# The first half of a retention and MLP kernel in rolling pairs of blocks, with 512-column first products

## The chip, the cores and the metric

The kernel runs on one core of one Trainium2 chip. The metric is the device time in microseconds, the median of three runs.

## The reference

Inputs q, k, v are (8, 8, 576, 64) in float32: 8 batches, 8 heads, 576 positions, 64 columns. The MLP has 512 inputs, 2048 hidden columns and 512 outputs.

```python
scores = q @ k.T / sqrt(64)                      # per batch and head
gamma  = 1 - 2 ** (-5 - head)
D      = gamma ** (i - j) where i >= j, else 0
attn   = (scores * D) @ v
x      = attn.transpose(0, 2, 1, 3).reshape(8 * 576, 8 * 64)   # (4608, 512)
h      = x @ w_in                                # (4608, 2048)
g      = maximum(h, 0) + alpha * minimum(h, 0)   # alpha per hidden column
out    = g @ w_out                               # (4608, 512)
```

The kernel must reach float32 accuracy. In the bulk of the work it gets there by splitting each float32 operand into three planes of a shorter format (`fp32r` in the profile), called planes 0, 1 and 2, and adding three products of planes.

## The kernel before

**Blocks, units, cells.** The 4608 tokens are 18 blocks (`kb`) of 256. The 2048 hidden columns are 8 units (`u`) of 256. A cell is one block by one unit: a first product (x by w_in, 512 deep, in four pieces `cc` of 128 and two halves `f` of 128 hidden columns), the activation with alpha, the split of g into planes, and a second product (g by w_out) that adds into PSUM. A visit is one block with four of the units; each block has two visits. The order is: blocks 0 to 15 with units 0 to 3 one block at a time (the first half), then blocks 16 and 17 in a pair, and then all blocks in pairs with units 4 to 7 (the second half). What the first visit of a block gives is stored to DRAM (`o_kept`, tile `ok`) and is added in the second.

**The start.** The first two batches' attention is computed with whole parts of q, k and v. The first eight cells (`unit_plain` L1073, `second_plain` L1104) work in plain float32 while the weights are loaded and converted (`convert`) and split (`split_w`).

**Attention beside the first half.** From the third batch on, attention goes by pairs of heads, 24 of them after the one of the start, one `joint` each. On TensorE a joint has the values of the pair before (L843, into `psh`) and the scores and state sums of its own pair (L895 and L902, L905, into `psh` and `psa`). Before it, `load_kq` and `load_kn` load q and k, `operands` scales them and turns them on VectorE (L821, into `kT` and `qT`; L826 scales `kn`). After it, VectorE masks the scores into `at` (L923) and forms the state sums (L937, L943, L946), and DMAs copy `qT` into `at` and the sums into `vn`. The x that comes out stays in a ring of five tiles `xs` and is stored to DRAM for the second visit (`fetch_x`). There are two rooms each of `kT`, `qT` and `kn`, and one of `kx`, `qx` and `at`.

**First half.** For a cell, `unit` makes per half `f` 12 matmuls of 256 columns (L1142) into one bank `psh[f]`: planes 0 and 1 into one half of the bank, plane 2 into the other. ScalarE and VectorE evacuate it in four steps into `ga` (L1149, L1150, L1153, L1156). `split_g` makes three planes of `ga` with two ScalarE (L1195, L1197) and two GpSimd passes (L1199, L1202). `second` makes 12 matmuls of 512 columns (L1275) into the four banks `pso`, two cells behind (`LAG`). `split_x` makes the planes of a block into one of two rooms `lx`, with four ScalarE and four GpSimd passes (L1030, L1045, L1048, L1052). Banks `psa` serve only the joints here.

**Second half.** `unit_two` makes the first product for two blocks at once: 12 matmuls of 512 columns (L1172) per half `f`, into the two banks `psh` for `f = 0` and `psa` for `f = 1`. It evacuates 512 columns at a time (L1178, L1179, L1182, L1184). The planes of x lie in the rooms that attention has left.

**The order of the work.** Every operation is recorded by `do` with its engine, a cost, what it reads and what it writes. Slots with a `Gen` for each use make an operation wait for all users of the room before. `plan` simulates the engines with these costs: first backwards for due times, then forwards, taking for each engine the ready operation that is due first. TensorE may run ahead in the recorded order by `AHEAD_PE` operations. The planner is called 144 times, 12 times on its own result and then with random changes to all due times, and the shortest plan is emitted. The order on each engine is then fixed; DMAs are nearly all issued on SP's queue (L208), in order, each waiting there for what it needs.

## Time and profile before

| what | value |
|---|---|
| median of 3 runs | 928.29 us (927.62 to 929.45) |
| profiled execution: span, first to last instruction | 926.8 us |
| profiled execution's own time | not listed apart; the span with 1.5 us around it is the median of the runs |
| mean granted TensorE clock | 0.999 |
| busy PE, PEld | 914.3 us (99%), 769.6 us (83%) |
| busy DVE, ACT, POOL | 521.1 us (56%), 542.6 us (59%), 601.9 us (65%) |
| DMA | 121.42 MB, mean 131 GB/s |
| L1142, first products of 256 columns | 1344 matmuls, 175.8 us busy |
| L1275, second products | 1608 matmuls, in two rows of 1392 and 216 |

PE is TensorE's matmuls, PEld its weight loads, DVE is VectorE, ACT is ScalarE, POOL is GpSimd, SP is the engine that issues DMAs. The profile gives times in microseconds, and the mean of one instruction in ns. Matmuls are pipelined, so that the mean of one is longer than the distance between two; for the distance take the length of a piece of the chain and divide by the number of matmuls. A row reads: line, engine, operation, output tile <- input tiles, shape, count, busy time, mean of one, and idle time before it with what ended it.

### The profile page before, as it was taken

Reading aid. Unit: us, or ns where it says so; the run is one execution under the profiler, and the core shown is the slowest. Engines: PE = TensorE matmul, PEld = TensorE weight load, DVE = VectorE, ACT = ScalarE, POOL = GpSimd, SP = SyncE. Lnnn points to the kernel's source line nnn. Section 1 sums busy time; section 2 is a strip of 40 time slices with the busy share of each in tenths; the row PEclk is TensorE's granted clock in tenths of the full one; section 3 lists DMA queues with packets and bytes.
Section 4 is the critical chain, followed back from the end, with each engine's and each line's share of the span. In section 5 each row is a group of like instructions: output and inputs, shape, how many; then the busy total and the mean of one; then the engine's idle time right before and its main releaser. Section 6 shows DMA issues by size and latency. Waiting matters only on the chain.

```text
span 926.8 us, 20611 instructions
## 1 busy us (share of the span) xinstructions
PE 914.3 (99%) x7913; PEld 769.6 (83%) x7913; DVE 521.1 (56%) x1043; ACT 542.6 (59%) x1164; POOL 601.9 (65%) x525
## 2 busy tenths in 40 slices
PE   7999999999999999999999999999999999999998
PEld 6666788888888888888988887888888888888886
DVE  7676666667676667666545454434454444443342
ACT  4566557567676667675856756545463646363442
POOL 4777856648776676674776678673756565565535
PEclk9999999999999999999999999999999999999999
DMA  9995687887988978964335231212121222311112
GB/s 225 247 228 105 168 190 156 197 192 167 205 209 201 212 172 207 197 148 134 116 123 165 86 114 45 92 46 92 46 91 58 80 82 76 106 56 47 46 46 68
DMA packets 235954, 121.42 MB, mean 131 GB/s; under 512 B 203456, under 2 KB 203728, under 8 KB 235856
## 3 DMA queue, kind: packets, MB, share of 16 engines
q1 hardware_dynamic: 235712, 119.98, 51.4%
q8 instruction: 62, 1.02, 0.5%
q14 instruction: 36, 0.29, 0.1%
q10 hardware_dynamic: 144, 0.13, 0.0%
HBM read 74.19 MB, written 32.51 MB: 115 GB/s over the span
## 4 chain that ended last, share of the span: by engine, by line
PE 92%; DMA 3%; DVE 1%; SPq 1%; POOL 1%; ACT 1%; issue 1%; POOLq 0%; ACTq 0%; DVEq 0%
PE pso L1275 39%; PE psh L1142 18%; PE psa L1172 11%; PE psh L1172 11%; PE psh L843 3%; PE pso L1104 2%; PE psh L1073 2%; PE psa L905 2%; SPq L208 1%; DMA w<-in_moe_w_out_dram 1%; PE psh L895 1%; PE psa L902 1%; DMA w<-in_v_dram 0%; DMA lx<-in_moe_w_in_dram 0%; DMA a<-in_moe_alpha_dram 0%
## 5 line engine op out<-in xcount | busy, mean ns | idle before, releaser
L1275 PE MATMUL pso<-w,g 128*128 128x512 f32 x1392 | 340.9, 391 | 0.6 <-POOL g L1202 0.6
L1275 PEld LDWEIGHTS pso<-w,g 128*128 128x128 f32 x1392 | 256.0, 188 | 51.5 <-POOL g L1202 1.2
L1202 POOL TENSOR_TENSOR g<-g 128x512 fp32r<-128x512 f32 x136 | 175.8, 1294 | 24.7 <-DVE w L1048 4.5
L1142 PE MATMUL psh<-lx,w 128*128 128x256 f32 x1344 | 175.8, 285 | 0.0
L1142 PEld LDWEIGHTS psh<-lx,w 128*128 128x128 f32 x1344 | 168.7, 191 | 6.9 <-issue 0.8
L1199 POOL TENSOR_TENSOR g<-ga,g 128x512 fp32r<-128x512 f32 x56 | 72.4, 1293 | 79.4 <-ACT g L1195 57.0
L1199 POOL TENSOR_TENSOR g<-x,g 128x512 fp32r<-128x512 f32 x48 | 62.2, 1296 | 73.7 <-ACT g L1195 55.7
L1149 ACT COPY ga<-psh 128x256 f32<-128x256 f32 x112 | 41.6, 372 | 57.2 <-PE psh L1142 54.4
L1199 POOL TENSOR_TENSOR g<-vn,g 128x512 fp32r<-128x512 f32 x32 | 41.5, 1295 | 40.5 <-ACT g L1195 34.3
L1150 DVE SCALAR_TENSOR_TENSOR ga<-psh,ga 128x256 f32<-128x256 f32 x112 | 47.2, 421 | 36.5 <-ACT ga L1149 34.5
L1156 DVE SCALAR_TENSOR_TENSOR ga<-psh,malpha,ga 128x256 f32<-128x256 f32 x112 | 53.4, 477 | 14.6 <-ACT psh L1153 14.0
L1153 ACT ACTIVATE psh<-ga 128x256 f32<-128x256 f32 x112 | 43.5, 388 | 22.6 <-DVE ga L1150 22.5
L1195 ACT ACTIVATE g<-x 128x512 fp32r<-128x512 f32 x48 | 30.3, 631 | 41.5 <-PE pso L1275 22.1
L1293 DVE TENSOR_TENSOR op<-pso,op 128x512 f32<-128x512 f32 x35 | 23.9, 687 | 52.9 <-PE pso L1275 52.9
L1275 PE MATMUL pso<-lx,g 128*128 128x512 f32 x216 | 52.0, 389 | 0.0
L1275 PEld LDWEIGHTS pso<-lx,g 128*128 128x128 f32 x216 | 40.5, 188 | 8.4
L923 DVE SCALAR_TENSOR_TENSOR at<-psa,pf,mask 64x512 f32<-64x512 f32 x48 | 36.0, 749 | 15.9 <-PE psa L902 14.9
L1195 ACT ACTIVATE g<-ga 128x512 fp32r<-128x512 f32 x56 | 35.4, 631 | 15.7 <-DVE ga L1156 14.7
L1048 POOL TENSOR_TENSOR lx<-x,lx 128x512 fp32r<-128x512 f32 x26 | 33.6, 1293 | 14.6 <-ACT lx L1045 9.8
L1179 DVE SCALAR_TENSOR_TENSOR x<-psh,x 128x512 f32<-128x512 f32 x24 | 16.5, 689 | 41.2 <-PE psh L1172 36.2
L1052 POOL TENSOR_TENSOR lx<-lx 128x512 fp32r<-128x512 f32 x28 | 36.2, 1294 | 2.5 <-DVE ga L1156 1.0
L843 PEld LDWEIGHTS psh<-at,vn 128*64 128x64 f32 x864 | 27.8, 137 | 10.6 <-issue 5.4
(311 smaller groups left out, 1842.4 us busy)
## 6 DMA issues: line engine op xcount, KB each, us to landing
xk<-x SPq DMA_DIRECT2D x18, 512.0 KB, 3.7
ok<-o SPq DMA_DIRECT2D x36, 256.0 KB, 2.6
op<-ok SPq DMA_DIRECT2D x18, 512.0 KB, 4.0
out_dram<-o SPq DMA_DIRECT2D x35, 256.0 KB, 2.3
x<-xk SPq DMA_DIRECT2D x16, 512.0 KB, 4.9
kx<-in_k_dram SPq DMA_DIRECT2D x96, 72.0 KB, 3.3
qx<-in_q_dram SPq DMA_DIRECT2D x96, 72.0 KB, 3.0
kn<-in_k_dram SPq DMA_DIRECT2D x48, 144.0 KB, 3.8
```

The source lines that it names most:

```text
L843: nc.tensor.matmul(pv[i].get()[half(h2), (j - js[0]) * C:(j - js[0] + 1) * C], vns[n % 2][:, h2, j], mt.get()[:, h2, j], start=True, stop= ...
L1052: lambda l=l, d=d, h=view(0, c): nc.gpsimd.tensor_tensor(out=piece(d()), in0=h(), in1=l(), op=ALU.subtract),
L1142: nc.tensor.matmul(at(b), w[:, c0:c0 + P], xp(l, cc), start=(n == 0 and cc == 0), stop=(n > 0 and cc == NCC - 1), skip_group_check=True)
L1149: do("ACT", 0.36, lambda g=g, at=at: nc.scalar.copy(g(), at(1)), [(ph, 1)], [(ga, f)])
L1150: do("DVE", 0.42, lambda g=g, at=at: nc.vector.scalar_tensor_tensor(out=g(), in0=at(0), scalar=ONE, in1=g(), op0=ALU.mult, op1=ALU.subtrac ...
L1153: do("ACT", 0.39, lambda g=g, at=at: nc.scalar.activation(at(1), g(), ACTF.Relu, scale=-1.0), [(ga, f)], [(ph, 1)])
L1156: do("DVE", 0.48, lambda g=g, at=at, fc=fc: nc.vector.scalar_tensor_tensor(out=g(), in0=at(1), scalar=malpha[:, fc:fc + 1], in1=g(), op0=A ...
L1172: nc.tensor.matmul(p.get(), w[:, c0:c0 + P], piece(words_of(g)[:, o:o + DM]), start=(l != 1 and cc == 0), stop=(l > 0 and cc == NCC - 1))
L1195: do("ACT", 0.64, lambda: nc.scalar.mul(piece(to.get()[:, 2]), whole(), BELOW), both, [(to, 2)])
L1199: do("POOL", 1.29, lambda: nc.gpsimd.tensor_tensor(out=piece(to.get()[:, 1]), in0=whole(), in1=to.get()[:, 2], op=ALU.subtract), both + [( ...
L1202: do("POOL", 1.29, lambda: nc.gpsimd.tensor_tensor(out=piece(to.get()[:, 2]), in0=to.get()[:, 0], in1=to.get()[:, 1], op=ALU.subtract), [( ...
L1275: nc.tensor.matmul(a[2 * m + b].get(), piece(g.get()[:, l, f, m * P:(m + 1) * P]), w_piece(u, 2 + f, l), start=(cell["first"] and f == 0 a ...
```

## The change

The blocks 2 to 15 of the first half go in rolling pairs. In step s (0 to 14) the blocks 1+s and 2+s are worked on with two units: units 0 and 1 in even steps, units 2 and 3 in odd ones. A block so gets two of its units as the newer one of a pair and two as the older one; in steps 0 and 14 there is one block alone. `unit_roll` makes the first product for both blocks at once, 512 columns per matmul, into `psh` for `f = 0` and `psa` for `f = 1`, in three operations of four matmuls. The two blocks' planes lie in one tile `lx` so that a matmul can take 256 columns of each with a fixed step between them. `split_roll` makes the planes with one ScalarE, one VectorE and one GpSimd pass per half of the block, and writes them into the room of the block two before. `acts_roll` evacuates 512 columns at a time.

`kT`, `qT` and `kn` get one room each, and `load_kn` moves from two pairs ahead to one. There are five rooms `ga` of 512 columns. The joints are placed by step (`JOINTS`). `split_g` has a second form (`quick`) with one ScalarE, one VectorE and one GpSimd pass, used in the last two steps, the first two pairs of the second half and at the very end. The later weight splits do one pass on VectorE in place of GpSimd (`WDVE`). The rooms of x and `ga` in the second half are chosen anew. The planner is called once, then 12 times on its own result, and then 243 times with random changes to the due times of operations within one stretch of 40 us at a time, keeping any plan that is no longer.

The core of the diff:

```diff
-    def plan(after=None):
-        after = after or [op.n for op in ops]
-
-        users = [[] for _ in ops]
+    users = []
+
+    def wait(d, op):
+        return 2.0 if d.late else 0.0 if d.eng == op.eng else LAT.get(d.eng, 0.1)
+
+    def dues(after):
...
+        return due
+
+    def plan(due):
...
+    WINDOWS, STRETCH, TRIES, ROUNDS = 27, 20.0, 9, 9
...
-    PUMP0, PUMP = ((1, 1), (0, 1), (0, 1), (0, 1)), ((1, 2), (1, 2), (0, 1), (0, 1))
+    X_TWO, QUICK, NQUICK, WDVE = 12, 13, 2, 16
+    PUMP_R = ((1, 1), (1, 1))
+    EARLY, JOINTS = 1, {(s, i): 1 for s in range(14) for i in range(2) if (s, i) not in ((0, 0), (8, 1), (10, 1), (13, 0), (13, 1))}
+    PUMP0, PUMP = ((1, 2), (0, 1), (0, 1), (0, 1)), ((1, 2), (1, 2), (0, 1), (0, 1))
...
-    lxs = [slot(lpool, f"lx{n}", [P, 3, NCC, TB]) for n in range(2)]
+    lx_tiles = {}
+
+    def lx_all(which):
+        if which not in lx_tiles:
+            lx_tiles[which] = lpool.tile([P, 6 * NCC, TB], FP32, tag="lx", name=f"lx_{which}")
+        return lx_tiles[which]
+
+    def lx_slots(which):
+        return [Slot(f"lx{n}", lambda n=n: lx_all(which)[:, 3 * NCC * n:3 * NCC * (n + 1)])
+                for n in range(2)]
+    lxs = lx_slots("w")
...
-    gas = [slot(mlp, f"ga{n}", [P, 2, TB]) for n in range(2)]
+    ga_all = mlp.tile([P, 5, DM], FP32, tag="ga", name="ga_all")
+    gas = [Slot(f"ga{n}", lambda n=n: ga_all[:, n].rearrange("p (f t) -> p f t", f=2)) for n in range(5)]
...
-    kns = [slot(nat, f"kn{n}", [P, NJ, D]) for n in range(2)]
-    kTs = [slot(attn, f"kT{n}", [P, S]) for n in range(2)]
-    qTs = [slot(attn, f"qT{n}", [P, S]) for n in range(2)]
+    kns = slot(nat, "kn", [P, NJ, D])
+    kTs = slot(attn, "kT", [P, S])
+    qTs = slot(attn, "qT", [P, S])
...
+        eng, cost, tt = ("DVE", 0.69, nc.vector) if at >= WDVE else ("POOL", 1.29, nc.gpsimd)
+        do(eng, cost, lambda: tt.tensor_tensor(
...
-    order = [(kb, (0, 1, 2, 3)) for kb in range(NKB - 2)]
+    order = [(kb, (2, 3, 0, 1) if kb % 2 and kb > 1 else (0, 1, 2, 3)) for kb in range(NKB - 2)]
...
-    def unit(cell):
...
+    def row_x(side, l):
+        return (3 * side + (l if side else 2 - l)) * NCC
+
+    def split_roll(vis):
+        fetch_x(vis)
+        x, side = vis["from"], vis["kb"] % 2
+        g = vis["x"] = Gen(lxs[side])
+        keys = [(x, *s) for s in x.keys]
+
+        def view(l, n):
+            r = row_x(side, l) + 2 * n
+            return lambda: lx_all("x")[:, r:r + 2]
...
+            do("ACT", 0.64, lambda n=n, h=h: nc.scalar.mul(piece(h()), raw(n), BELOW * 2.0 ** -12),
+               keys, [(g, 0, n)])
+            do("DVE", 0.70, lambda n=n, h=h, l=l: nc.vector.scalar_tensor_tensor(
+                out=piece(l()), in0=h(), scalar=-2.0 ** 12, in1=raw(n), op0=ALU.mult, op1=ALU.add),
+                keys + [(g, 0, n)], [(g, 1, n)], lock=True)
+            do("POOL", 1.29, lambda h=h, l=l, d=d: nc.gpsimd.tensor_tensor(
+                out=piece(d()), in0=h(), in1=l(), op=ALU.subtract),
+                [(g, 0, n), (g, 1, n)], [(g, 2, n)], lock=True)
...
+    def unit_roll(some, u, f, fine):
+        sides = [vis["kb"] % 2 for vis in some]
+        wide = len(some) == 2
+        cols = slice(0, DM) if wide else slice(sides[0] * TB, (sides[0] + 1) * TB)
+        p0, p1 = (Gen(x) for x in (psa if f else psh))
 
         def xp(l, cc):
-            g, o = at_x[l, cc]
-            return piece(words_of(g)[:, o + side * TB:o + (side + 1) * TB])
-        ga = Gen(gas[cell["n"] % 2])
-        for f in range(2):
-            ph = Gen(psh[f])
-
-            def at(b, ph=ph):
-                return ph.get()[:, b * TB:(b + 1) * TB]
-
-            def mm(f=f, at=at):
-                for n, (b, l) in enumerate(((0, 0), (1, 2), (0, 1))):
+            r = [row_x(side, l) + cc for side in sides]
+            t = lx_all("x")[:, r[0]:r[1] + 1:r[1] - r[0]] if wide else lx_all("x")[:, r[0]]
+            return piece(t)
+
+        def out_of(p):
+            t = p.get()[:, cols]
+            return t.rearrange("p (s t) -> p s t", s=2) if wide else t
+        for some_l in (((p0, 0),), ((p0, 1),), ((p1, 2),)) if fine else (
+                ((p0, 0), (p0, 1), (p1, 2)),):
+            def mm(some_l=some_l):
+                for p, l in some_l:
                     for cc in range(NCC):
                         w = w_piece(u, cc // 2, l)
                         c0 = (cc % 2 * 2 + f) * P
-                        nc.tensor.matmul(at(b), w[:, c0:c0 + P],
-                                         xp(l, cc), start=(n == 0 and cc == 0),
-                                         stop=(n > 0 and cc == NCC - 1), skip_group_check=True)
-            do("PE", 1.43, mm, x_keys(vis, side) +
-               [w_at[u, i][l] for i in range(2) for l in range(3)], [(ph, 0), (ph, 1)], size=24, kind="pieces")
...
+                        nc.tensor.matmul(out_of(p), w[:, c0:c0 + P], xp(l, cc),
+                                         start=(l != 1 and cc == 0), stop=(l > 0 and cc == NCC - 1))
+            ls = [l for _, l in some_l]
+            do("PE", (0.911 if wide else 0.483) * len(ls), mm,
+               [(vis["x"], l, n) for vis in some for l in ls for n in range(2)] +
+               [w_at[u, i][l] for i in range(2) for l in ls],
+               [(p, 0) for p in (p0, p1) if any(p is q for q, _ in some_l)], size=8 * len(ls), kind="pieces")
+        return p0, p1, out_of
+
+    def acts_roll(ps, gens, g, u, f):
...
+        if quick[0]:
+            do("ACT", 0.64, lambda: nc.scalar.mul(piece(to.get()[:, 0]), whole(), BELOW * 2.0 ** -12),
+               both, [(to, 0)])
+            do("DVE", 0.70, lambda: nc.vector.scalar_tensor_tensor(
+                out=piece(to.get()[:, 1]), in0=to.get()[:, 0], scalar=-2.0 ** 12, in1=whole(),
+                op0=ALU.mult, op1=ALU.add), both + [(to, 0)], [(to, 1)], lock=True)
+            do("POOL", 1.29, lambda: nc.gpsimd.tensor_tensor(
+                out=piece(to.get()[:, 2]), in0=to.get()[:, 0], in1=to.get()[:, 1], op=ALU.subtract),
+                [(to, 0), (to, 1)], [(to, 2)], lock=True)
+            return
...
+            load_kn(x + 1)
-            load_kn(x + 2)
...
-    ga_rooms = [xs[2], xs[3], xs[4]]
-    nga = [3]
...
+    big_rooms = [[Gen(None), t] for t in (vns[0], vns[1], None, ga_all[:, 0:2], ga_all[:, 2:4])]
+    nga = [0]
...
+    for _ in range(EARLY):
+        joint_(next(todo))
+    split_roll(visits[2])
+    last = singles - 1
+    t = 8
+    for s in range(last):
+        some = [visits[kb] for kb in (1 + s, 2 + s) if 2 <= kb <= last]
+        us = (0, 1) if s % 2 == 0 else (2, 3)
+        now_cells = {(vis["n"], u): c for vis in some for c in of[vis["n"]] for u in us if c["u"] == u}
+        queue += [now_cells[vis["n"], u] for vis in some for u in us]
+        quick[0] = s >= QUICK
+        by_side = sorted(some, key=lambda vis: vis["kb"] % 2)
+        if s == 0:
+            split_roll(visits[3])
...
+        for i, u in enumerate(us):
+            cs = [now_cells[vis["n"], u] for vis in by_side]
+            gens, g = take_rooms(cs)
+            for f in range(2):
+                for _ in range(ahead.get(t, 0)):
+                    convert((op_, 0), was, None)
+                t += 1
+                ps = unit_roll(by_side, u, f, True)
+                acts_roll(ps, gens, g, u, f)
+                if f:
+                    for c, ga in zip(cs, gens):
+                        c["ga"] = ga, ga.get
+                    ahead_g()
+                pump(PUMP_R[i][f])
+                if f:
+                    for _ in range(JOINTS.get((s, i), 0)):
+                        joint_(next(todo))
+                if i and f and 3 + s <= last and s:
+                    assert NPAIR * (ready_kb[3 + s] + 1) in done
+                    split_roll(visits[3 + s])
+        if s == X_TWO:
+            next_x(visits[16])
+            next_x(visits[17])
+        if s == last - 2:
+            split_first(16)
+            split_first(17)
+    pump(1)
+    ahead_g(3)
...
-    best = made = plan()
+    due = dues([op.n for op in ops])
+    best = made = plan(due)
+    for _ in range(12):
+        again = dues(made[3])
+        made = plan(again)
+        if made[0] < best[0]:
+            best, due = made, again
     rng = np.random.RandomState(1)
-    for n in range(144):
-        if n < 12:
-            made = plan(made[3])
-        else:
-            made = plan(list(best[3] + rng.uniform(-1, 1, len(ops)) * (0.5, 2.0, 5.0)[n % 3]))
-        best = min(best, made, key=lambda x: x[0])
+    for n in range(ROUNDS * WINDOWS):
+        lo = STRETCH * (n // TRIES % WINDOWS)
+        some = [i for i, t in enumerate(best[2]) if lo <= t < lo + 2 * STRETCH]
+        other = list(due)
+        for i, x in zip(some, rng.uniform(-1, 1, len(some)) * (1.0, 3.0, 9.0)[n % 3]):
+            other[i] += x
+        made = plan(other)
+        if made[0] <= best[0]:
+            best, due = made, other
```

## The prediction

> **What bounds the kernel now.** I read the page's busy time and chain first, then the stages by window, then the groups by shape, and last the pieces of the chain and the tiles that change rooms. The first fence has whole lines of the page: busy time, and the chain by engine and line.
>
> ```profile
> PE 914.3 (99%) x7913; PEld 769.6 (83%) x7913; DVE 521.1 (56%) x1043; ACT 542.6 (59%) x1164; POOL 601.9 (65%) x525
> PE 92%; DMA 3%; DVE 1%; SPq 1%; POOL 1%; ACT 1%; issue 1%; POOLq 0%; ACTq 0%; DVEq 0%
> ```
>
> The end is set by TensorE; the other 8% of the chain is nearly all start-up. The next fence has the stages (the columns are the stretch, its length, and busy time of PE, PEld, DVE, ACT, POOL). From 103.3 us, where the narrow first products (L1142) begin, to 482.75 us, where the wide ones (L1172) begin, PE is never idle, and DVE, ACT and POOL stay below 69%.
>
> ```profile
> 103.30:482.75 379.45, 379.45 (x4436) 336.52 (x4435) 251.28 (x563) 253.96 (x608) 260.22 (x210) 1.00 0.76 178
> 482.75:927.00 444.25, 439.71 (x1942) 363.58 (x1941) 196.01 (x319) 231.80 (x451) 272.66 (x242) 1.00 0.24 76
> ```
>
> After the start, the list of PE's waits has one entry, 0.6 us for a GpSimd split at 563 us. So the first half is priced by how long PE's instructions take in a row. The chain in order of time shows that (start, length, what); the first four lines are from the first half, the last two from the second:
>
> ```profile
> 209.05 2.86 PE psh L1142 x24
> 211.92 1.39 PE pso L1275 x6
> 216.13 0.61 PE psh L843 x16
> 216.74 1.59 PE pso L1275 x6
> ...
> 482.75 2.72 PE psh L1172 x12
> 485.47 1.36 PE pso L1275 x6
> ```
>
> A cell (one block of 256 tokens by one unit of 256 hidden columns) takes 24 narrow matmuls, 2.87 us in most pieces: 119.5 ns each. Twelve wide ones, 512 columns for two cells, take 2.72 us: 226.7 ns each. Six second products take 1.39 us after narrow ones, 1.36 us among wide ones, 1.59 us just after attention's small matmuls.
>
> **The change part by part.** *First products.* The 1344 narrow matmuls are 14 blocks x 4 units x 24. The rolling scheme has 15 steps of two units: 13 with two blocks (13 x 2 x 2 x 12 = 624 wide) and two with one (96 narrow). Before: 1344 x 0.1195 = 160.6 us. After: 624 x 0.2267 + 96 x 0.1195 = 141.5 + 11.5 = 153.0 us. That takes off 7.6 us, all of it on the path.
>
> Two things bear on 226.7 ns. The wide operand is now two runs of 256 columns with a gap (two blocks' rows of one tile), and before.py has no such moving operand. The nearest rows bound it: 226.7 ns as one run, 2 x 119.5 = 239.0 ns as two matmuls; below 226.7 is excluded, since as many columns go through. The upper end costs 624 x 12.3 = 7.7 us, the whole gain. I take the lower: the instruction count is that of one wide matmul, and it is the instruction that the narrow row pays for (2 x 119.5 - 226.7 = 12.3 ns for the second one). The Trainium skill (TensorE: Matmul & The Clock Gate, Back-to-back issue gap) gives columns / 2.4 GHz + about 2.5 ns for an isolated matmul, so that a pair would save only 2.5 ns and the step 1.6 us, an estimate from that page; the rows here differ, and they decide.
>
> *Second products.* After wide instead of narrow ones, a piece loses about 0.03 us (1.39 against 1.36). I count 83 second-product pieces on the chain of this stage; not all follow narrow ones. I take 1.5 us off, between 0 and 2.5.
>
> *Restarts after small matmuls.* 1.59 - 1.39 = 0.2 us each; joints (24) and their grouping stay. Nothing.
>
> *Evacuation.* The narrow chain is ACT 372, DVE 421, ACT 388, DVE 477 ns, 112 times each. The wide one (psh rows) is 580, 689, 602, 749 ns, 52 times, and the narrow one is left 8 times. ACT: 85.1 to 67.6 us. DVE: 100.6 to 82.0 us. Off the path.
>
> *Splitting x.* Per half block, two ACT and two POOL passes become ACT 0.63, DVE 0.69, POOL 1.29 us. Over 28 halves ACT drops by some 17 us, POOL by 26 x 1.293 = 34 us, and DVE gains 28 x 0.69 = 19 us. With evacuation DVE ends about where it was (251 + 1 of 379 us). Covered by PE's products; if DVE were late, who waits is priced next.
>
> *New waits.* Three rooms get tighter; before shows no such wait.
> (a) lx. Block s+3 is split into the plane room of block s+1, whose last reader is the last product of step s. The first plane is there after two ACT passes, 1.26 us, the last after 0.63 + 0.69 + 2 x 1.29 = 3.9 us; its product starts 1.8 us into the unit. PE has between them a ready second product (2.72 us) and, in all of these steps but 8 and 10, a joint: 30.1 us of L843 over 24 plus some 1.2 us of scores and sums = 2.45 us. Without a joint 0 to 1.2 us stands open, more if the split queues on DVE. Queued behind it are the next unit's products.
> (b) psa. It now holds half of the first products besides scores and sums. Room time per joint: product 2.7 us; evacuation 2.4 to 3.8 us (in the second half's timeline, from the product's end to the end of L1184); small matmuls 1.1 us; masks and sums 2.6 to 4.8 us (the joint at 233.5). In sum 8.8 to 12.4 us, of a period of 4 x 2.72 + 2.45 = 13.3 us. It fits, with 0.9 to 4.5 us over.
> (c) One kT, qT and kn. The load of kn for joint x+1 can start only when joint x is over: two issues of 0.65 us on SP, landing 3.8 us (at most 5.5), ACT 0.78 us: 5.9 us, 7.6 at worst, against 13.3. qT is free when its copy into at has landed (3.2 us after issue), then two transposes of 0.77 us. SP and its followers (loads of q and k, stores) queue behind the kn load while it waits.
>
> ```profile
> L821 DVE STREAM_TRANSPOSE kT<-kx x24: 734/769/780, 72.7 to 406.4; 128x576 f32<-128x576 f32 x24
> L902 PE MATMUL psa<-qT,kT x768: 218/218/218, 98.6 to 428.3; 64*64 64x64 f32 x192
> DMA to landing us min/median/max: 2.8/3.8/5.5
> ```
>
> The first line (tile kT: durations in ns, first and last start) against the second shows how far operands run ahead now: 21 to 26 us before their joint, nearly two periods. One room cuts that to under one period; the third line (tile kn) is what must then fit. All three are 0 at the lower end; a gain is excluded, since PE waits for none of them now. Blocks 4 to 15 are split so, 12 times; the upper end is 12 x 1.2 us = 14 us for (a). I take 2.5 us in all, some 0.1 us for each of 24 joints, because each room's own sum fits its period.
>
> *Banks in turn.* The Trainium skill (TensorE: Matmul & The Clock Gate, A second HAM failure mode: psum-queue depth-cycling) warns that going round PSUM banks lets PE pause between groups and the clock fall. Here the second half already alternates psh and psa, at a granted clock of 1.00 in every window to 900 us. So the sum has no term for it; by the rule it would have a loss of a size that no row gives.
>
> *Second half and planner.* Some 22 splits of g go from two ACT and two POOL passes to one each plus DVE 0.69 us, and 16 weight passes from POOL 1.29 to DVE 0.69 us: 26 us more on DVE, which is busy 196 of 444 us. PE's 0.6 us wait for POOL may go. A different search gives another order; in the stage at full PE it can find only the 0.2 us restarts, and in the first 103 us, where DMA is in the chain, I allow 2 us either way and take 0.
>
> **The sum.** Span 926.8 - 7.6 - 1.5 + 2.5 = 920.2 us. The profiled execution's span is 1.5 us under the median of the runs (928.29); with these 1.5 us around it, 921.7 us.
>
> **The rivals.**
> 1. *Operands late (slower).* The kn load, behind other work in SP's order, or the copy of qT makes the joint late; PE's order is fixed, so it stands. From 0.4 us for each of 23 joints (9.1 us) the gain is gone. Landing at its worst each time costs 23 x 1.7 = 39 us; I price a third, 13 us: 928.3 - 9.1 + 13 = 932 us. For it: the loss of lead, and DMA engines busy 76% in this stage. Against: 5.9 us in a 13.3 us period.
> 2. *The split or the banks eat the gain.* (a) and (b) at about two thirds of 14 us, 10 us: 928.3 - 9.1 + 10 = 929 us. For it: 0.9 us over in the worst psa sum. Against: ACT and POOL are relieved by some 34 us each.
> 3. *Two runs cost like two matmuls*, so that nothing is widened: 921.7 + 7.7 = 929 us. Against: same number of instructions as wide.
>
> **How the numbers follow.** The main case 0.66, rival 1 0.20, rival 2 0.09, rival 3 0.05. A measurement can tell about 0.2% (1.9 us) from no change. Faster takes the main case, 0.66; rivals 2 and 3 lie on the line and give 0.09 same and 0.05 slower, so that slower is 0.25 with rival 1. Low end: 928.3 - 7.6 - 2.5 - 0.6 - 2 = 915.6, no new wait. High end 932, up to rival 1's price. The main case alone: 915.6 to 926.
>
> **What would show it.** Right: 624 matmuls of 128x512 at some 227 ns apart in place of most L1142; the wide products beginning the second stage some 7 us earlier; PE's waits still near nothing. Wrong: pieces of 12 wide ones at 2.87 us (rival 3); PE waiting for ACT kn, DVE kT or DMA at the scores (rival 1), or for POOL lx or DVE on psa and psh at first products (rival 2). A gain beyond 13 us would mean the start or the second half moved, which I don't forecast.

## The result, and the profile after

The changed kernel's median is 926.20 us (21 runs, 921.56 to 930.57), against 928.68 us for the kernel before beside it (21 runs, 927.14 to 932.35). The ratio is 0.9969, interval 0.9956 to 0.9981: faster by 0.31%, 2.5 us, where 6.6 us were forecast. In two later comparisons, each beside the kernel before, the same kernel gave 0.9951 and 0.9937. The profiled execution took 921.56 us, the quickest of the 21, with a span of 919.6 us and so 2.0 us around it. It shows what this order of operations can do, not what it mostly does; a second profile, of an execution of 924.69 us, is read beside it below.

First the busy time of the page of after, then the groups by shape (line, engine, operation, tile and shape, count, busy time and mean ns, idle before).

```profile
PE 909.4 (99%) x7289; PEld 737.3 (80%) x7289; DVE 547.3 (60%) x1003; ACT 505.2 (55%) x1010; POOL 519.5 (56%) x461
...
L1187 PE MATMUL psh<-lx_x,w 128*128 128x512 f32 x312 | 80.2, 395 | 0.0
L1187 PE MATMUL psa<-lx_x,w 128*128 128x512 f32 x312 | 77.8, 390 | 0.0
```

There are 624 wide first products, and 624 fewer matmuls in all (7913 to 7289). The mean of 390 ns is not the distance, since matmuls overlap; that is in the timeline of after (start, length, what), at one group of 16:

```profile
203.34 1.07 PE L1187 MATMUL psh<-lx_x,w 128*128 128x512 f32 x4
204.24 1.07 PE L1187 MATMUL psa<-lx_x,w 128*128 128x512 f32 x4
205.15 1.07 PE L1187 MATMUL psh<-lx_x,w 128*128 128x512 f32 x4
206.06 1.07 PE L1187 MATMUL psa<-lx_x,w 128*128 128x512 f32 x4
206.96 1.52 PE L1339 MATMUL pso<-w,g 128*128 128x512 f32 x6
```

Sixteen starts in 3.62 us are 226 ns each: the two-run operand costs what a single run of 512 columns costs.

Now the stages, by window: the start, the first half from its first product, the second half from its first product (stretch, length, busy time and number of PE, PEld, DVE, ACT and POOL instructions). First those of after, in its 921.56 us execution.

```profile
0.00:104.33 104.33, 98.94 (x1641) 72.01 (x1642) 80.89 (x176) 58.36 (x110) 68.02 (x74) 1.00 0.85 193
104.33:472.27 367.94, 367.35 (x3702) 301.03 (x3701) 243.91 (x465) 217.50 (x454) 215.50 (x176) 1.00 0.77 176
472.27:919.60 447.33, 443.14 (x1950) 364.26 (x1948) 222.49 (x363) 229.36 (x446) 235.99 (x213) 1.00 0.25 82
```

The same stages of before, with the same marks. Its first narrow product starts at 102.74 us, while the product ahead of it still runs; the prediction's 103.30 us is where the chain passes to it. The mark of after is such a start too.

```profile
0.00:102.74 102.74, 94.61 (x1538) 69.17 (x1538) 73.26 (x162) 56.88 (x105) 68.47 (x74) 1.00 0.88 197
102.74:482.59 379.85, 379.85 (x4437) 336.68 (x4435) 251.84 (x563) 253.81 (x608) 260.62 (x211) 1.00 0.76 178
482.59:926.80 444.21, 439.87 (x1943) 363.74 (x1941) 196.01 (x319) 231.95 (x452) 272.82 (x242) 1.00 0.24 76
```

And those of the changed kernel run again, in its execution of 924.69 us:

```profile
0.00:106.08 106.08, 98.94 (x1641) 72.11 (x1642) 79.89 (x176) 58.18 (x110) 67.78 (x74) 1.00 0.84 190
106.08:475.57 369.49, 369.00 (x3703) 301.56 (x3702) 244.20 (x465) 216.69 (x454) 215.93 (x176) 1.00 0.76 175
475.57:922.70 447.13, 442.95 (x1950) 364.24 (x1948) 222.47 (x363) 229.44 (x446) 236.25 (x213) 1.00 0.26 82
```

Lengths alone mislead, because work moved over the marks; the counts say how much. By their starts, the start has 104 matmuls more: one joint now lies there (36 of the values, L860, and 68 of scores and sums), 2.45 us by the prediction's price. Six second products have moved from the first half to the second, 6 x 0.227 = 1.36 us. (A window's count also has those that only reach into it, so it can differ by one to three.) So from before and the prediction's terms alone, with no new wait, the stages should be:

| stage | should be, us | after | again |
|---|---|---|---|
| start | 102.74 + 2.45 = 105.19 | 104.33 | 106.08 |
| first half | 379.85 - 2.45 - 1.36 - 7.65 - 1.5 = 366.89 | 367.94 | 369.49 |
| second half | 444.21 + 1.36 = 445.57 | 447.33 | 447.13 |

So against this sum the first half lost 1.1 to 2.6 us to something new, the second half 1.6 to 1.8 us, and the start went either way. Yet the list of PE's waits after the start holds nearly nothing (after):

```profile
PE psa L922 <- DVE ga_all L1207: 0.4, 1, 0.4
PE pso L1283 <- POOL g L1255: 0.2, 1, 0.2
```

Matmul records are longer (390 ns) than the distance between two (227 ns), so of each delay the first 0.16 us or so leaves no idle time in the record. To find such losses I compared the distances from one start to the next, matmul by matmul, between profiles with the same order.

### The profile page after: what moved, and what is told of

Read it like the earlier page. It is cut to its first block, busy times and chain, and to the rows that moved or that the text cites. A ratio compares the mean times of both kernels' runs of the same rounds, so it can differ in the third digit from the quotient of the medians.

```text
span 919.6 us, 19101 instructions
## 1 busy us (share of the span) xinstructions
PE 909.4 (99%) x7289; PEld 737.3 (80%) x7289; DVE 547.3 (60%) x1003; ACT 505.2 (55%) x1010; POOL 519.5 (56%) x461
## 5 line engine op out<-in xcount | busy, mean ns | idle before, releaser
L1263 POOL TENSOR_TENSOR g<-ga_all,g 128x512 fp32r<-128x512 f32 x76 | 98.0, 1291 | 121.9 <-ACT g L1259 93.9
L1266 POOL TENSOR_TENSOR g<-g 128x512 fp32r<-128x512 f32 x114 | 147.3, 1293 | 16.6 <-DVE w L1065 4.4
L1187 PE MATMUL psh<-lx_x,w 128*128 128x512 f32 (+1 forms) x360 | 87.4, 381 | 0.0
L1187 PE MATMUL psa<-lx_x,w 128*128 128x512 f32 (+1 forms) x360 | 84.5, 375 | 0.0
L1187 PEld LDWEIGHTS psh<-lx_x,w 128*128 128x128 f32 x360 | 63.9, 188 | 13.9 <-issue 0.5
L1187 PEld LDWEIGHTS psa<-lx_x,w 128*128 128x128 f32 x360 | 64.7, 188 | 12.6 <-ACT kn L843 0.3
L1259 ACT ACTIVATE g<-ga_all 128x512 fp32r<-128x512 f32 x76 | 47.7, 631 | 41.6 <-PE pso L1339 21.8
L1162 POOL TENSOR_TENSOR lx_x<-lx_x 128x512 fp32r<-128x512 f32 x28 | 35.8, 1288 | 39.8 <-DVE lx_x L1159 36.9
L1255 POOL TENSOR_TENSOR g<-g 128x512 fp32r<-128x512 f32 x22 | 28.4, 1293 | 46.7 <-DVE g L1252 29.6
L940 DVE SCALAR_TENSOR_TENSOR at<-psa,pf,mask 64x512 f32<-64x512 f32 x48 | 36.0, 749 | 31.5 <-PE psa L919 27.1
L1339 PE MATMUL pso<-lx_x,g 128*128 128x512 f32 x216 | 53.3, 390 | 0.1
L1261 ACT ACTIVATE g<-ga_all 128x512 fp32r<-128x512 f32 x76 | 47.2, 621 | 1.2 <-PE pso L1339 1.0
L1339 PEld LDWEIGHTS pso<-lx_x,g 128*128 128x128 f32 x216 | 40.4, 188 | 9.0 <-DVE o L1362 0.7
L860 PEld LDWEIGHTS psh<-at,vn 128*64 128x64 f32 x864 | 27.8, 137 | 10.0 <-issue 6.0
L1221 PE MATMUL psh<-w,w 128*128 128x512 f32 x144 | 34.6, 389 | 0.0
```

What stands on the lines that cost most here:

```text
L860: nc.tensor.matmul(pv[i].get()[half(h2), (j - js[0]) * C:(j - js[0] + 1) * C], vns[n % 2][:, h2, j], mt.get()[:, h2, j], start=True, stop= ...
L940: nc.vector.scalar_tensor_tensor(out=mt.get()[half(1 - h2), h2, j], in0=fro[x], scalar=pf[x, 1, h:h + 1], in1=mask[x, None, :].to_broadcas ...
L1162: do("POOL", 1.29, lambda h=h, l=l, d=d: nc.gpsimd.tensor_tensor(out=piece(d()), in0=h(), in1=l(), op=ALU.subtract), [(g, 0, n), (g, 1, n) ...
L1187: nc.tensor.matmul(out_of(p), w[:, c0:c0 + P], xp(l, cc), start=(l != 1 and cc == 0), stop=(l > 0 and cc == NCC - 1))
L1221: nc.tensor.matmul(p.get(), w[:, c0:c0 + P], piece(words_of(g)[:, o:o + DM]), start=(l != 1 and cc == 0), stop=(l > 0 and cc == NCC - 1))
L1255: do("POOL", 1.29, lambda: nc.gpsimd.tensor_tensor(out=piece(to.get()[:, 2]), in0=to.get()[:, 0], in1=to.get()[:, 1], op=ALU.subtract), [( ...
```

## The experiments

They ask four things: is the widening worth its 7.65 us; what do the tighter rooms and the kn loads cost; what does the planner's order do; and what happens in the start. A version with two rooms for kn, the direct undo of that part, was not run.

**The changed kernel again.** No edit; it gives the runs that the next ones are read against.

> The changed kernel once more, unchanged, for a second profile. The first profile is of an execution of 921.56 us, the shortest of 21 (median 926.2 us), and in it TensorE has next to no waits. Theory A (operands late): an ordinary execution, about 926 us, shows 3 to 6 us of waits of TensorE at the scores and sums (L912, L919, L922) that the first profile does not have, released by ACT kn, DVE kT or DVE qT. Theory B (planes or banks late): the same amount at the first products (L1187), released by POOL or DVE on lx_x or by DVE on ga_all. Theory C (outside the rolling stage): the second half's wide products begin at the same 472 us as in the first profile, and the time is lost before 104 us or after 472 us.

924.44 us (923.23 to 924.69), before 929.15; ratio 0.9951 (0.9937 to 0.9964). Its stages are those above. PE's list after the start has only two waits of 0.2 us, so neither theory A nor B shows as expected. The second half begins at 475.57 us, 3.3 us later than in the first profile: 1.75 us of it is the start, 1.55 us the first half.

**First products narrow again, in the same order.**

```diff
-  nc.tensor.matmul(out_of(p), w[:, c0:c0 + P], xp(l, cc), ...)
+  for e in range(len(some)):      # one matmul of 256 columns for each block
+      o = sides[e] * TB
+      nc.tensor.matmul(p.get()[:, o:o + TB], w[:, c0:c0 + P], piece(t), ...)
```

> Each wide first product of the rolling stage becomes two of 256 columns, one for each block, into the two halves of the same bank; planner costs and so the order on every engine are as in the changed kernel. It measures the widening alone. If the term of the sum was right (624 x 12.3 ns = 7.7 us), the span from the first to the last first product of that stage grows by 7 to 8 us and the time by as much, to about 933.5 us. If the two-run operand costs as much as two matmuls, nothing changes, 926 us. If TensorE is not what bounds the stage in an ordinary execution, the time grows by clearly less than 7 us, since waits shrink in exchange.

931.69 us; ratio 0.9951 became 1.0036 (1.002 to 1.0052). That is 7.25 us over the changed kernel beside it. The groups by shape and the windows of this version:

```profile
L1190 PE MATMUL psh<-lx_x,w 128*128 128x256 f32 x672 | 90.5, 285 | 0.0
...
103.90:480.59 376.69, 375.43 (x4326) 334.44 (x4325) 244.11 (x466) 217.61 (x454) 216.39 (x176) 1.00 0.74 172
480.59:927.90 447.31, 443.04 (x1950) 364.33 (x1948) 222.47 (x363) 229.45 (x446) 236.27 (x213) 1.00 0.26 82
```

The first half is 7.2 us longer than in the run above and the second half the same: in this order the whole gain of the change is in the width of these matmuls. All else that it does costs time here: 0.36% over before when the width is taken back (on another order, below, 0.00%).

**kn loaded no more from the third joint on, in the same order.** The planner still sees the loads; they are left out when the instructions are issued. The room is scaled again each time, so the state sums are of other data.

```diff
+  if n > 9: kn.get = loaded[9][2].get
-  [(kn, h2)], rate=RATE_256)
+  [(kn, h2)], rate=RATE_256, skip=n > 9)
```

> kn is loaded for the first two joints only, and later joints use what is in its room (it is scaled again each time), so that the state sums are of other data; the plan and the order on every engine are those of the changed kernel, without 46 of the issues on SP. Theory A (operands late): ACT's waits for the landing of kn (16.4 us in the first profile) go, and the time falls by 3 to 5 us, to 921 to 923 us, with a smaller spread. Theories B and C: within 1 us of the changed kernel, 925 to 927 us.

920.06 us (919.45 to 922.3); 0.9911 (0.9894 to 0.9927), 4.4 us under the changed kernel. The first half of this version, and ScalarE's waits for kn (us in total, times, longest), first here, then in the changed kernel run again:

```profile
104.50:470.66 366.16, 366.16 (x3702) 300.81 (x3701) 243.79 (x465) 216.71 (x454) 215.62 (x176) 1.00 0.66 159
```

```profile
ACT kn L847 <- DMA kn<-in_k_dram: 3.1, 2, 2.7
```

```profile
ACT kn L843 <- DMA kn<-in_k_dram: 17.5, 11, 3.6
```

The first half is 366.16 us, 0.7 us under the sum with no wait (366.89 us); the second half, 447.04 us, is not shorter. So, in this order, what the first half loses is the work of the kn loads: against this run 1.8 us in the quick profile of the changed kernel and 3.3 us in the run again.

**kn loaded, but nobody waits for it.** As in the run just above, with the loads issued at the same places into a DRAM tile that is not read; again the sums are of other data.

```diff
+  kn_away = dram.tile([P, NJ, D], FP32, tag="kaway", name="kaway")
-  [(kn, h2)], rate=RATE_256)
+  [(kn, h2)], rate=RATE_256, skip=(lambda h2=h2: kn_away[half(1 - h2)]) if n > 9 else False)
```

> Order as in the changed kernel. From the third joint on, the loads of kn go to a place in DRAM that nobody reads: SP issues as many of them with as many bytes read, but ScalarE no longer waits for them and SP no longer waits for kn's room (the sums are of other data, as in the run with kn loaded once). Theory A2 (the waits in ScalarE's queue cost 4.4 us in this order): the time stays where it was without the loads, 920 to 921 us, about 0.991 of the kernel before. If the traffic or the issues on SP are what costs: back to 924 us, about 0.995.

924.35 us (921.83 to 927.62); 0.9945 (0.9924 to 0.9967), as the changed kernel. ScalarE's waits for kn fall as without the loads, but the first half does not:

```profile
108.90:477.95 369.05, 367.39 (x3703) 301.33 (x3702) 244.07 (x465) 217.00 (x454) 215.84 (x176) 1.00 0.74 175
```

```profile
ACT kn L849 <- DMA kn<-in_k_dram: 2.9, 1, 2.9
```

So neither ScalarE's wait for kn nor the single room takes the time, but that the transfers run or are issued. The intervals of this ratio and the last just touch; the verdict rests on the first half, 369.05 against 366.16 us.

The two profiles also show a way from the loads to PE. In this run ScalarE waits for other loads instead: for pieces of the weights (`op`) that it converts, 8.6 us in the first half against 3.4 us without the kn loads. At the largest place, ScalarE's timeline here, then the same copy of psa without the loads, then PE's waits here:

```profile
408.54 0.66 ACT L735 ACTIVATE op<-op 128x512 int32<-128x512 uint32 x1 [3.44 <-DMA op<-in_moe_w_out_dram]
409.65 0.56 ACT L1207 COPY ga_all<-psa 128x512 f32<-128x512 f32 x1
```

```profile
402.24 0.59 ACT L1205 COPY ga_all<-psa 128x512 f32<-128x512 f32 x1 [0.58 <-PE psa L1191]
```

```profile
PE psa L928 <- DVE ga_all L1213: 0.7, 1, 0.7
PE psh L866 <- DMA vn<-su: 0.6, 2, 0.3
```

The two issues of kn take SP's queue from 399.78 to 402.01 us. The load of the weights comes next, at 402.12 us, and lands 6.4 us later; without the kn loads it is issued at 395.79 us and lands in 4.2 us. Counted from the first product, it lands 4.2 us later, and the copy that empties psa, queued on ScalarE behind the conversion, begins 3.1 us later. The joint that needs psa (L928), the values of the same joint, which wait for the copies of the state sums (`vn`), and the second product after them lose 2.7 of the 2.9 us that this first half has over the run without the loads. At the same place the changed kernel's three profiles lose 1.4 of 1.8 us, 1.1 of 3.3 us and 0.9 of 3.4 us; ScalarE stands there 1.0 to 1.3 us for kn and 0.7 to 1.0 us for `op`. The copies into `vn` land in 3.3 to 3.4 us (median) with the kn loads and in 2.4 us without. This is read from the traces; no run moved the loads of the weights alone.

**kn scaled on GpSimd**, planned anew.

```diff
-  nc.scalar.activation(t, t, ACTF.Copy, scale=tabk[:, c:c + 1])      # ACT
+  nc.gpsimd.tensor_tensor(out=t, in0=t, in1=tabk[:, c:c + 1, None]..., op=ALU.mult)   # POOL
```

> kn is scaled by GpSimd in place of ScalarE (the same product with tabk, 1.15 us in the planner); its load and its one room stay, and the order is planned anew. Theory A1 (the joint itself stands because kn lands late): nothing gained, 924 to 927 us, since kn is ready no sooner. Theory A2 (ScalarE waits for the landing, 17.5 us in all in the profile of the changed kernel, and the evacuation queued behind it is late): the waits for the landing move to GpSimd, which is busy 58% of the stage, ScalarE is free of them, and the time falls by 2 to 4 us against the changed kernel, to about 0.992 of the kernel before.

924.82 us, before 928.3; 0.9960 (0.9945 to 0.9975). The wait goes to GpSimd (18.1 us in ten pieces in its list) and the time stays.

**The planner told that kn's load takes 2 us more.**

```diff
-  return 2.0 if d.late else ...
+  return 2.0 + d.slow if d.late else ...      # d.slow = 2.0 for the kn load
```

> The planner takes 2 us more from the issue of a load of kn to its use (4.7 instead of 2.7 us; the landing was 3.6 us at the median); nothing else is changed, the order is planned anew. Theory A2: ScalarE's scale comes later in its order, its waits for the landing fall from 17.5 us to under 5 us, and the time falls by 2 to 4 us against the changed kernel, to about 0.992 of the kernel before. If ScalarE's waits go and the time stays, A2 falls.

926.96 us; 0.9983 (0.9971 to 0.9994). ScalarE now waits for kn only once, 1.4 us, and the kernel is no faster. But this order and that of the GpSimd version were planned anew, and other seeds alone move the time by as much as the expected 2 to 4 us (below), so these two do not refute theory A2. The run with the loads sent to DRAM does, for the wait for kn; that ScalarE's waits for other loads hold up what is queued behind them is what the traces above show.

**The new search on the kernel before.** Only `dues`, `plan(due)` and the loop of 12 + 243 plans.

> The kernel before, with only the planner's search exchanged for the one by stretches; all operations are as before. Prediction: the order changes, the time does not, 926 to 930 us against 928.7 us. Theory C, that the search gives or takes away time by itself: it moves by 2 us or more, in either direction, and then the changed kernel's gain is not the widening's alone.

931.35 us; 1.0019 (1.0004 to 1.0034): it moved by 2.2 us, so theory C's sign came, towards slower.

**The old search on the changed kernel.** The reverse edit.

> The changed kernel with the planner's search of before (144 plans, random changes to all due times). The search by stretches alone cost 2 us on the kernel before. Theory C (the search gives time away): about 2 us less than the changed kernel, 0.993 of the kernel before. Otherwise the search of before finds a worse order for the tighter rooms and it is slower than the changed kernel, 0.997 or more.

924.85 us; 0.9946 (0.9928 to 0.9964), as with the new one, and between the two expectations. The new search brings no gain on either kernel.

**Another seed for the search of the changed kernel.**

```diff
-  rng = np.random.RandomState(1)
+  rng = np.random.RandomState(2)
```

> The changed kernel with another seed of the planner's random search: the same operations, another order of the same quality in the planner's own terms. It shows how much of a difference of any planned-anew kernel is the order's luck. If luck is small, within 1 us of the changed kernel (0.995 of the kernel before); if it is 2 us or more, single differences of that size say nothing about a cause.

920.21 us (918.39 to 920.85); 0.9903 (0.9888 to 0.9919): nearly 1% under before, some 4 us under the changed kernel, and the best version found. Its windows:

```profile
0.00:104.80 104.80, 98.30 (x1641) 71.94 (x1642) 78.92 (x171) 58.32 (x110) 69.07 (x75) 1.00 0.87 191
104.80:474.92 370.12, 369.82 (x3715) 303.53 (x3713) 246.23 (x474) 217.85 (x458) 214.80 (x175) 1.00 0.77 177
474.92:918.80 443.88, 439.89 (x1937) 362.24 (x1935) 220.72 (x360) 227.80 (x443) 236.12 (x212) 1.00 0.24 81
```

It has 12 second products more in the first half than the first order has, and 12 fewer in the second. With 12 x 0.227 us added, the first half should be 366.89 + 2.72 = 369.61 us: this order loses 0.5 us there, not 1.1 to 2.6.

**Seed 2 without the kn loads**, as above on the other order.

> kn loaded for the first two joints only, on the order of seed 2 (0.9903 of the kernel before, with 9.7 us of ScalarE's waits for kn against 14 to 17.5 us in the changed kernel). If the landing of kn is what parts the two orders, there is little left to gain here: within 1.5 us of seed 2, 0.989 to 0.991. If the load of kn costs some 4 us in any order, it falls to 0.986.

919.82 us; 0.9909 (0.9886 to 0.9933). In this order the loads cost nothing that can be told from zero (its one profile has a first half 0.9 us shorter).

**Seed 2 with narrow first products.**

> Wide first products of the rolling stage as two of 256 columns, on the order of seed 2 (920.2 us). If the widening's worth does not depend on the order: 7 to 8 us more, 927 to 928.5 us, so that this order without the widening is level with the kernel before.

929.36 us; 1.0000 (0.9983 to 1.0017). Against 0.9903 the width is worth 0.97%, 9.0 us, on this order, a little over the expected 7 to 8. In its profile PE waits 1.5 us for the copies of the state sums (`vn`), which the wide version does not, so not all of it is the width itself.

**Seeds 3 and 4 of the changed kernel.**

> The changed kernel with a third seed of the search. Orders of it have given 0.990 to 0.998 of the kernel before. Theory L (order's luck: some 0.4% either way around a true gain of about 0.5 to 0.6%): between 0.990 and 0.998, and the kernel before has luck of the same size.

923.72 us; 0.9944 (0.9925 to 0.9962).

> The changed kernel with a fourth seed. Theory L: 0.990 to 0.998 of the kernel before, with the mean over its orders at about 0.994, that is 7 us under the mean over the orders of the kernel before (about 1.0016) and not 2.5 us.

925.13 us; 0.9976 (0.9966 to 0.9986).

**Seeds 2 and 3 of the old search of the kernel before.**

> The kernel before with seed 2 of its search. Theory L: another order of the kernel before moves it as orders of the changed kernel do, by 2 us or more in either direction (the search by stretches moved it by 2.2 us). If only the changed kernel with its single rooms is so touchy, it stays within 1 us of the kernel before.

931.47 us; 1.0029 (1.0014 to 1.0043).

> The kernel before with a third seed of its search. Theory L (order's luck, with the kernel before's own order a lucky one): 1 to 4 us slower than the kernel before, 1.001 to 1.004. If its own order is nothing special, within 1 us of it.

928.00 us; 1.0006 (0.9997 to 1.0014).

By seed, the changed kernel's time is thus some 0.7% wide (0.9903 to 0.9976) and that of the one before 0.3%. The own order of the one before is the quickest of its three, though the third seed cannot be told from it, so that it is a lucky one is not shown. The changed kernel's own order (0.9969, 0.9951 and 0.9937 in three comparisons) is in the middle of its four. Means over the orders, each with its kernel's own search: 0.9944 and 1.0012, so 0.68% or 6.3 us apart. With four orders against three that is rough, and no interval is claimed.

Much of this width does not lie in the rolling pairs. With the moved matmuls counted as above, the first halves of seeds 3 and 4 lose 0.6 and 1.0 us in their profiles, hardly more than seed 2; but their starts take 109.2 us, against 104.8 us (of seed 3's, 1.8 us are four plain second products more). The start of seed 4:

```profile
0.00:109.20 109.20, 100.60 (x1641) 74.00 (x1642) 79.65 (x172) 58.08 (x110) 68.88 (x75) 0.97 0.84 187
```

PE stands there once for 2.87 us with no releaser in the profile, and the granted clock of the start is 0.97 (0.98 with seed 3, 1.00 with seed 2). All eleven runs of seed 4 have a mean granted clock of 0.995 to 0.998; the 22 runs of before beside them have 0.997 to 1.0.

**The changed kernel a third time.**

> The changed kernel, unchanged, beside these three on the same chip: 923 to 926 us, with the wait at 30 us in its profile if the profiled execution is one of its longer ones.

923.17 us (921.84 to 927.13), before 929.47; 0.9937 (0.9914 to 0.996). First half 369.59 us (103.80 to 473.39). The profiled execution, 922.27 us, is a quick one and has no wait at 30 us. Here two of the small waits came to light in PE's list:

```profile
PE psh L1187 <- DVE at L940: 0.9, 1, 0.9
PE pso L1339 <- DVE o L1362: 0.6, 1, 0.6
```

**Fewer loads in flight, and more.** The planner limits the bytes in flight in the first 100 us.

```diff
-  LIMITED, IN_FLIGHT = 100.0, 5 << 18
+  LIMITED, IN_FLIGHT = 100.0, 3 << 18      # and 8 << 18
```

> The changed kernel with at most 3 instead of 5 quarter-megabyte loads in flight on SP's queue in the first 100 us; order as in the changed kernel. Theory S (start): the fetch of TensorE's instructions at 27 us (one packet of 16 KB, seen at 26.9 us in a quick execution, at 29.4 and 30.7 us in two slow ones) is late behind the loads in flight, which gives the 2.5 to 3 us wait at 30 us in some executions. Then with less in flight the fetch is in time, the wait is gone in every execution and the spread of the times shrinks to about 2 us; the median falls by up to 2 us, unless the loads themselves come late, which would show as waits for DMA before 100 us and cost some us.

934.33 us (933.51 to 937.2); 1.0056 (1.0036 to 1.0075). PE now waits for loads, and the spread is 3.7 us, not the 2 us expected:

```profile
PE psa L651 <- DMA w<-in_k_dram: 2.5, 1, 2.5
```

> The same with 8 in flight. Theory S: the fetch is late more often and by more; the wait at 30 us is in the profile, and the median rises by 1 to 3 us. If the wait does not depend on the loads in flight, the time stays within 1 us of the changed kernel.

927.66 us; 0.9979 (0.9962 to 0.9995), 4.5 us over the changed kernel beside it. PE's list here has three waits that no other engine ends:

```profile
PE psh L598 <- issue: 1.9, 1, 1.9
PE psh L1404 <- issue: 1.7, 1, 1.7
...
PE psh L525 <- issue: 1.7, 1, 1.7
```

## Why the prediction was right or wrong

**First products: right.** Forecast 7.65 us; taking the width back in an unchanged order cost 7.25 us, and about 9 us on the order of seed 2. The Trainium skill (TensorE: Matmul & The Clock Gate, Back-to-back issue gap) put 2.5 ns on each isolated matmul, which by an estimate from that page would have made this step 1.6 us; the trace's 12.3 ns a pair decided rightly. Rival 3 (two runs cost like two matmuls) is ruled out by the 226 ns.

**Second products and restarts: right with the kn loads away.** In the distances between matmuls the steps that start at a second product are 236.2 ns each in before, 235.4 ns in after and 234.2 ns without the loads: 0.5 us for 648 of them in the changed kernel, 1.3 us without the loads, where 1.5 us were taken. The loads' delays ate most of it again. The first half without the loads is 0.7 us under the sum, because the first products gained a little more than their term: from start to start, their small gaps included, they take 164.5 us in before and 156.1 us without the loads, 8.4 us less.

**New waits: the size right, the path to them wrong.** I took 2.5 us, "some 0.1 us for each of 24 joints, because each room's own sum fits its period". Against the sum the first half lost 1.1 us in the quick profile, and 2.2 to 2.7 us in the three others with the kn loads (369.05, 369.49 and 369.59 us against 366.89). That the size fits is in part luck, since the waits are not where the sums by rooms looked. Rival 1 would have PE wait for kn, kT or qT; it waited for none of them. kn was scaled at least 1.8 us ahead of its scores, mostly 2.7 us and more, though mostly 15 to 24 us in before. What was late, when the matmuls of the profiles are laid side by side, came in a few pieces of 0.1 to 1.0 us, not at every joint: scores and sums waiting for DVE to empty psa (L922 behind L1207), values waiting for the copies of the state sums (`vn`, L860), second products behind POOL's split of g (L1266) or DVE's sum into o (L1362), first products behind DVE's masks (L940) or POOL's split of x (L1162). Most of these are rival 2's kind of wait, at well under its price of 10 us. But their source lies nearer to rival 1, "the kn load, behind other work in SP's order", turned round: other work behind the kn load. The prediction had written that "SP and its followers (loads of q and k, stores) queue behind the kn load", and gave it no price. That the kn loads cause the loss in this order is shown by the run without them; the way over the late load of the weights and ScalarE's queue is seen in the traces at the largest place. How much is due to the issues and how much to the traffic stays open.

**Second half, planner and start: the step that failed.** The prediction had "PE's 0.6 us wait for POOL may go" and "in the stage at full PE it can find only the 0.2 us restarts", and took 0 for the second half, for the order and for the start. For the second half the five profiles with this order give 447.0 to 447.7 us against 445.57: 1.5 to 2.1 us more, every time. In PE's distances (after) that is 1.0 us behind DVE: the quick split of g (L1252, near 508 us) and the sum into o (L1362, near 516 and 904 us). Another 1.2 us is behind POOL: the quick split at the end (L1255, near 910 us) and, 0.16 us each at five places from 596 to 902 us, the long split (L1266). The one wait that before has there, at 563 us, is gone in return. The 26 us of work moved to DVE (196 to 222 us busy) was called covered, because DVE is half idle; it is covered but for the pieces behind it. No run took these steps back, so this too is read from the traces.

For the run again the terms close: forecast was a span of 920.2 us, measured are 922.7 us. Of the 2.5 us between, the first half has some 0.1 us (2.6 us lost where 2.5 us were allowed), the second half 1.6 us and the start 0.9 us.

For the order, 0 was wrong in both directions: seeds alone move the changed kernel by 0.7% from best to worst (0.9903 to 0.9976, 6.8 us), as much as the whole forecast gain. The comparison drew a middling order of the changed kernel against the best known of the kernel before. The 0.68% between the means of the orders happens to equal the forecast of 0.7%; the terms that were missed, the second half above all, do not make that a confirmation.

**The start: the range of 2 us was too narrow.** With the joint moved in, 105.19 us were due. The five profiles with this order have 103.8, 104.3, 104.5, 106.1 and 108.9 us: from 1.4 us better to 3.7 us worse, by execution and not by order. The median of the first comparison lies 4.6 us above its own profile. Which stage took those runs longer is not known, as only one of them was profiled; the spread of the start is the candidate.

**What would show it: held.** 624 wide matmuls 227 ns apart; the wide products of the second half beginning 7.0 to 10.3 us earlier in the changed kernel's three profiles; and, after the start, no wait near a microsecond in the first profile. But "PE's waits still near nothing" was a poor sign: it held, and 1.1 to 2.6 us were lost in the first half all the same, since of each delay the first 0.16 us does not show as idle time. The depth-cycling that the Trainium skill warns of (TensorE: Matmul & The Clock Gate, A second HAM failure mode: psum-queue depth-cycling) did not come: psh and psa now alternate in the first half too, and the granted clock is 1.00 in the windows of both halves.

## What to carry to other kernels

Where matmuls overlap, the number of instructions times their distance in the chain gave a good price (7.65 forecast, 7.25 measured), and an empty list of waits gave a false comfort: compare the stages' lengths after correcting for work that moved over their marks by the counts, and put the marks at the same event in both. Where a planner writes the order, one order of each version is one draw: here seeds moved the time by 0.7%, more than the change itself, so try a few seeds of both before a difference of this size is put down to the change, and keep the best. When a load moves in a DMA queue that goes in order, price what stands behind it, not only the load and its own room. An engine that is half idle still does not cover a step on the path of a buffer that PE needs next.

## What the runs showed of the hardware that was not expected

The start of one and the same program differs between executions. In the run again PE stands still for 2.55 us in the midst of the small matmuls of L598, with nothing it waits for; in the first profile of the changed kernel it does not. The timeline of the run again, then the windows from 24 to 34 us of the run again and of after:

```profile
29.75 0.22 PE L598 MATMUL psh<-w,w 64*64 64x64 f32 x1
32.52 0.27 PE L598 MATMUL psh<-w,w 64*64 64x64 f32 x1 [2.55 <-issue]
```

```profile
24.00:34.00 10.00, 7.02 (x203) 5.48 (x203) 9.44 (x17) 5.13 (x10) 6.44 (x7) 1.00 1.09 238
```

```profile
24.00:34.00 10.00, 9.58 (x217) 6.62 (x216) 9.44 (x18) 6.96 (x13) 6.46 (x7) 1.00 1.07 258
```

The 16 DMA engines are full in both (share 1.07 to 1.09). In the trace's DMA records a 16 KB packet of an instruction queue (q8) starts at 27.01 us in the first profile and at 26.85 us in the run without the kn loads, both of which have no such wait; it starts at 29.36 us in the run again, and at 30.68 us in the run with kn loaded into DRAM, which waits 3.0 us. With eight loads in flight there are three such waits, 1.7 to 1.9 us each; with three in flight none, though a packet starts at 29.55 us there too, and the loads then come late and cost more. That PE's instructions wait behind the loads in the same DMA engines would fit most of this; neither was the fetch moved by itself nor is it shown whose queue this is, so it is not shown.

Some of these stands come with a lower clock. In the run with kn loaded into DRAM the granted clock is 0.50 from 34.1 to 37.5 us, just after the 3.0 us; with seed 4 it is 0.50 from 24.4 to 27.8 us, around the end of its 2.87 us. In the run again, after 2.55 us, it stays at 1.00.
